# Query and output projections as three products of 16-bit halves instead of one fp32 product

## The chip, the cores and the metric

The kernel runs on one core of one Trainium2 chip. The metric is the device time of one execution in microseconds (us); lower is better. The numbers come from three timed runs of the kernel before and from one profiled execution, whose trace lists every instruction of the engines: PE (TensorE, with PEld for its weight loads), DVE (VectorE), ACT (ScalarE), POOL (GpSimd) and SP (SyncE, which here only issues DMAs).

## The reference

Two independent blocks are computed from separate inputs and joined on the last axis: block A, a state-space convolution over 2048 positions and 576 channels, and block B, attention with 32 query heads of 18 columns that share one key head and one value head. The change touches the first and the last matrix product of block B.

```python
def _B_ref(x, wq, wk, wv, wo):            # x (1, 2048, 576), wq and wo (576, 576), wk and wv (576, 18)
    ...
    q = (lambda x, *d: x.transpose(*d))((x @ wq).reshape(B, S, H, Dh), 0, 2, 1, 3)
    k = x @ wk
    v = x @ wv
    scores = jnp.einsum("bhqd,bkd->bhqk", q, k) * (Dh ** -0.5)
    p = _softmax(scores, axis=-1)
    o = jnp.einsum("bhqk,bkd->bhqd", p, v)
    return (lambda x, *d: x.transpose(*d))(o, 0, 2, 1, 3).reshape(B, S, H * Dh) @ wo
...
a = _A_ref(...)                            # kernel of 2048 taps per channel, FFT convolution, plus u * Dskip
return jnp.concatenate([a, b], axis=-1)
```

## The kernel before

**Attention.** The 2048 queries are cut into four chunks of 512 (`c`), and the 32 heads into 16 pairs (`pr`). For each chunk, two pairs form a group (`g`), and for each group the 2048 keys are walked in 16 blocks of 128 (`kb`). One step of this walk is one score tile of 128 keys by two heads of 512 queries: `scores` (L509) makes it with two 16-bit matmuls, `exponentials` (L520) turns it into `P` with one ACT instruction of 1024 elements, and `product` (L816) multiplies two such `P` tiles by the values into `ops`, in fp32. There are 1024 score tiles, and so 1024 exponentials. Score tiles have three PSUM buffers, so the scores of tile i+3 wait for the exponential of tile i. After a group, `gather` (L530) copies `ops` to SBUF and stores it to DRAM.

**Query projection.** `side` (L691) goes through 20 units (chunk c, block m of 128 query columns; the last block has 64). Unit (0, 0) is made during setup. Each other unit is `qproj` (L394): five blocks k of the 576 rows of `wq`, each for two halves of 256 queries, and for each four matmuls in fp32, one for each group of 32 output columns; the four run side by side in the array. In the trace one fp32 matmul is two passes, each with a weight load of its own (the program has 680 of these matmuls, the trace 1360). The result lies in the single PSUM bank of tag `f`, which every other piece of side work shares. DVE takes it out as `qh` and `ql`.

**Output projection.** When a chunk's eight groups are stored, `prepare` (L711) runs `normalize` (L538): denominators `dn` are loaded, inverted on DVE and stored to DRAM (`rden`), the chunk's numerators are loaded into `oT`, and for each block m of 126 rows the inverses are loaded broadcast into `db` (two buffers) and multiplied into `oT` by one DVE instruction. `outproj` (L574) then makes eight tiles (t, n) of 128 x 288, each a sum over five blocks m in fp32. The last chunk is done in parts: `outproj_part` (L600) as far as it gets beside the attention, and `finish` (L625) for what is left in `self.rest` after the last exponential.

**Convolution.** Class `Conv` makes block A in 12 chunks of 48 channels on DVE and PE: `front(k)` builds the filter (`tab`, `kg`, `ksb`), `back(k)` transforms input and filter (`hu`, `lu`, `hk`, `lk`), multiplies them (`ks`, `acc`, `pt`, `sv`, `w`) and transforms back (`iy`). Its DVE work is the larger part of what DVE does.

**What sets the order.** The order of PE, ACT and DVE is laid down while the program is built. `Clock` (L76) keeps an estimated time for each of the three engines; `Vector` (L111) and `K.pe(...)` add an estimated cost for each instruction issued. Between the scores and products of a round of three tiles, `fill` (L785) takes pieces of side work from three streams (normalization `prep`, projections `side`, convolution `conv`) as long as a credit lasts and their inputs are due. `self.due` forces a query unit in time for the heads that need it. The convolution is paced by `RATE` (1.84 us of DVE work for each step of two tiles), and what is left of it when the last exponential is issued is written out by `conv.drain()` (L894), behind everything else. Each engine then executes its list strictly in that order, whatever the real durations are.

## Time and profile before

| | us |
|---|---|
| median of three runs | 1151.15 |
| lowest and highest of the three | 1151.06, 1153.36 |
| span of the profiled execution, first to last instruction (its own time is not listed apart from the three) | 1153.0 |
| mean granted TensorE clock | 0.990 |
| first exponential starts | 26.9 |
| last exponential starts | 1127.2 |

Three things are needed to read it. The exponentials are a ruler: 1024 of them, of about 1 us each, so a stretch between two of them is a fixed part of the attention's work, and what lies behind the last one is the tail. PE's busy time counts each matmul to the end of its way through the array, so that matmuls that follow each other overlap, and busy PE is not PE at its peak. DVE executes in order, one instruction at a time, and its records overlap their neighbours by less than a tenth of a microsecond.

### The profile page before, as it was taken

To read this page: it belongs to the slowest core of one execution; us is meant where nothing else is said; L and a number is where in the kernel's file an instruction comes from. 1 tells how busy PE (TensorE), PEld (TensorE's weight loads), DVE (VectorE), ACT (ScalarE), POOL (GpSimd) and SP (SyncE) were. 2 spreads that over 40 slices of the span, in tenths; PEclk is the share of its full clock that TensorE was granted. 3 is DMA by queue.
4 is the path that set the end of the run, shared out by engine and by line. 5 is a ranking of instruction groups with operands and counts; after the bars stand their busy time and mean duration, and the time that the engine had idled before them with its cause. 6 is when DMAs were issued, how large, how long until landed. Compare 5 with 4: busy or idle time off the path is not lost.

```text
span 1153.0 us, 33012 instructions
## 1 busy us (share of the span) xinstructions
PE 1083.5 (94%) x13886; PEld 395.9 (34%) x13886; DVE 987.4 (86%) x1679; ACT 998.8 (87%) x1052; POOL 140.6 (12%) x257
## 2 busy tenths in 40 slices
PE   6999899989999999989999999999998999999998
PEld 2333233333333334323333333333332333332423
DVE  3697997998997897897799899898699799799694
ACT  2888979879989898998998899988999988899891
POOL 5232320112032000001021200001040000000000
PEclk9899999999999999999999999999999999999999
DMA  7422242114122202112222300202221301301201
GB/s 224 130 57 84 76 133 89 45 41 135 32 67 78 74 29 88 45 63 93 82 79 71 110 21 28 93 28 85 75 78 46 111 20 39 106 19 54 77 33 58
DMA packets 59279, 83.37 MB, mean 72 GB/s; under 512 B 14867, under 2 KB 35335, under 8 KB 58613
## 3 DMA queue, kind: packets, MB, share of 16 engines
q1 hardware_dynamic: 47557, 73.24, 19.4%
q0 software_dynamic: 10848, 7.37, 2.6%
q8 instruction: 111, 1.82, 0.6%
q10 hardware_dynamic: 720, 0.58, 0.2%
q14 instruction: 43, 0.35, 0.1%
HBM read 46.59 MB, written 33.85 MB: 70 GB/s over the span
## 4 chain that ended last, share of the span: by engine, by line
PE 64%; DVE 15%; ACT 14%; issue 5%; DMA 1%; SPq 0%; ACTq 0%; DVEq 0%
PE ops L823 27%; PE s L516 17%; ACT P L527 12%; PE op L193 5%; PE q L408 3%; DVE tab L119 3%; PE kg L1257 3%; PE iy L193 3%; DVE ks L119 1%; DVE acc L119 1%; DVE t L119 1%; PE hk L193 1%; PE fin L193 1%; PE lk L193 1%; DMA xr<-xT 1%
## 5 line engine op out<-in xcount | busy, mean ns | idle before, releaser
L527 ACT ACTIVATE P<-s 128x1024 f32<-128x1024 f32 x992 | 934.8, 1034 | 104.6 <-PE s L516 102.2
L823 PE MATMUL ops<-P,v_sb 128*32 128x512 f32 x4096 | 513.0, 601 | 8.5 <-DVE o L123 8.4
L516 PE MATMUL s<-aug,kaug 55*128 55x512 f16 x2048 | 309.9, 384 | 36.6 <-ACT P L527 30.7
L516 PEld LDWEIGHTS <-kaug 55*128 55x128 f16 x2048 | 92.2, 94 | 371.7 <-issue 328.5
L823 PEld LDWEIGHTS ops<-P,v_sb 128*32 128x32 f32 x4096 | 117.2, 110 | 162.6 <-issue 126.1
L458 POOL DMA_DIRECT2D qd<-qh x116 | 65.7, 573 | 323.2 <-DVE qh L127 320.6
L408 PE MATMUL q<-x,wq_sb 128*32 128x256 f32 x1360 | 84.2, 382 | 3.2 <-DVE sck L119 2.5
L193 PE MATMUL op<-wo_sb,oT 126*32 126x288 f32 (+1 forms) x1048 | 74.8, 410 | 2.6 <-DVE sck L119 1.2
L119 DVE TENSOR_TENSOR tab<-tab,tt 128x576 f32<-128x576 f32 (+1 forms) x72 | 59.1, 821 | 1.4
L123 DVE COPY ksb<-kg 128x192 f32<-128x192 f32 x48 | 17.5, 364 | 49.1 <-PE kg L1257 48.9
L119 DVE TENSOR_TENSOR tt<-fr,sum 128x576 f32<-128x576 f32 (+1 forms) x72 | 58.9, 818 | 0.0
L119 DVE TENSOR_TENSOR tab<-tab 128x576 f32<-128x576 f32 (+1 forms) x72 | 58.9, 818 | 0.0
L119 DVE TENSOR_TENSOR tab<-fr,dif 128x576 f32<-128x576 f32 (+1 forms) x72 | 58.9, 818 | 0.0
L119 DVE TENSOR_TENSOR tab<-sum,fr 128x576 f32<-128x576 f32 (+1 forms) x72 | 58.8, 816 | 0.0
L408 PEld LDWEIGHTS q<-x,wq_sb 128*32 128x32 f32 x1360 | 40.5, 110 | 43.4 <-issue 19.1
L1168 POOL MEMSET fr<- 128x192 f32 x24 | 9.8, 494 | 323.8 <-DVE tt L119 225.2
L119 DVE TENSOR_TENSOR acc<-acc,pt 128x1728 f32<-128x1728 f32 (+2 forms) x36 | 48.7, 1352 | 0.3
L119 DVE TENSOR_TENSOR pt<-us,ks 128x1728 f32<-128x1728 f32 (+2 forms) x36 | 48.2, 1351 | 0.0
L525 ACT ACTIVATE P<-s,bias 128x1024 f32<-128x1024 f32 x32 | 32.7, 1131 | 15.1 <-PE s L516 15.1
L193 PEld LDWEIGHTS op<-wo_sb,oT 126*32 126x32 f32 (+1 forms) x1048 | 29.8, 110 | 42.2 <-issue 17.4
L1257 PEld LDWEIGHTS kg<-tab 128*32 128x32 f32 x2304 | 35.5, 110 | 22.9 <-issue 7.9
L1257 PE MATMUL kg<-tab 128*32 128x64 f32 x2304 | 41.8, 221 | 1.5 <-DVE ksb L123 1.1
(160 smaller groups left out, 1018.0 us busy)
## 6 DMA issues: line engine op xcount, KB each, us to landing
od<-o SPq DMA_DIRECT2D x31, 256.0 KB
aug<-qd SPq DMA_DIRECT2D x124, 55.0 KB
u<-u SPq DMA_DIRECT2D x12, 384.0 KB
kd<-ksb SPq DMA_DIRECT2D x12, 384.0 KB
kt<-kd SPq DMA_DIRECT2D x48, 96.0 KB
outa<-u SPq DMA_DIRECT2D x12, 384.0 KB
pw<-pw SPq DMA_DIRECT2D x8, 528.0 KB
oT<-od SPq DMA_DIRECT2D x16, 252.0 KB
```

Of the source, the lines that this page charges most:

```text
L119: return self.v.tensor_tensor(out, *a, **k)
L123: return self.v.tensor_copy(out, *a, **k)
L193: nc.tensor.matmul(ps[j:e], w[:, j:e], x, start=start, stop=stop, tile_position=(0, j))
L408: nc.tensor.matmul(ps[o, 256 * f:256 * f + 256], w[:, k, i], xt[:, k, x], start=(k == 0), stop=(k == 4), tile_position=(0, 32 * j))
L458: q.dma_start(qd[h:h + n, row + d:row + d + nd, cs], src[i1:i1 + n * nd, :cs.stop - cs.start])
L516: nc.tensor.matmul(ps[:, j, :], self.kaug[r, kb * P:(kb + 1) * P], t[r, :], start=True, stop=True)
L525: nc.scalar.activation(pt, ps, AF.Exp, bias=self.bias, scale=SCALE / QQ)
L527: nc.scalar.activation(pt, ps, AF.Exp, scale=SCALE / QQ)
L823: nc.tensor.matmul(o_ps[32 * j:32 * j + 32, :], self.v[:, kb, :], pts[2 * n + j // 2][:, j % 2, :], start=(kb == 0), stop=(kb == 15), tile ...
L1168: nc.gpsimd.memset(t[:, :, 0:NF:8], one)
L1257: nc.tensor.matmul(ps[32 * g:32 * g + 32, d, :], t[:, :32], t[:, 32:], start=(j == 0), stop=(j == 1), tile_position=(0, 32 * g))
```

## The change

Both operands of the two projections are split into a 16-bit high half and a 16-bit low half (the rest after the high half is taken away), with scales `XS`, `WS` and `OS` that are taken back when the result leaves PSUM. The fp32 product becomes three 16-bit products: high x high, high x low and low x high. The halves are made on DVE by `split`, one multiplication and one subtraction for each piece; the subtraction also writes a sum, from which `guard` later decides whether the fast path is to be believed (beside the bound that was tested before).

```diff
+    def stage(self, src, name):
+        rows, n = src.shape[0], math.prod(src.shape[1:])
+        t = self.p1.tile([P, CT], F32, tag="st", name=name, bufs=2)[:rows, :n]
+        self.nc.sync.dma_start(t if len(src.shape) == 2 else t.rearrange("p (k n) -> p k n", k=src.shape[1]), src)
+        return t, self.k.t + 5.0
+
+    def split(self, src, scale, hi, lo, part=None):
+        V, n = self.V, self.summed
...
+        V.tensor_scalar(hi, src, scale, None, op0=ALU.mult)
+        V.scalar_tensor_tensor(lo, src[part], scale, hi[part], op0=ALU.mult, op1=ALU.subtract,
+                               accum_out=self.sums[part.start:part.start + src[part].shape[0], n:n + 1])
...
+    def split_x(self, c):
...
+            st = {k: self.stage(a[:, k, :], f"xs{c}_{k}") for k in range(2)}
+            for k in range(5):
+                src, ready = st[k]
+                yield "v", max(ready, self.k.t), False
+                if k < 4:
+                    self.split(src, XS, t[:, k, :], t[:, 4 + k, :])
+                else:
+                    self.split(src, XS, t[:, 8, :], t[64:, 8, :], slice(64, P))
...
     def qproj(self, c, m, xt):
-        w, nf = self.wq[m], 2 if m < 4 else 1
...
+        w, n = self.wq[m], CT if m < 4 else 256
+        terms = [x for k in range(4) for x in ((k, k), (k, 4 + k), (4 + k, k))] + [(8, 8), (9, 8)]
...
-        for f in range(nf):
-            for k in range(5):
+        for i0 in cuts:
+            part = range(i0, min(i0 + size, len(terms)))
+            for i in part:
                 for j in range(4):
...
-                    nc.tensor.matmul(ps[o, 256 * f:256 * f + 256], w[:, k, i], xt[:, k, x], start=(k == 0), stop=(k == 4), tile_position=(0, 32 * j))
-                K.pe(0.465)
...
+                    nc.tensor.matmul(ps[o, :n], w[:, terms[i][0], wc], xt[:, terms[i][1], x], start=(i == 0), stop=(i == len(terms) - 1), tile_position=(0, 32 * j))
+            K.pe(0.02 + 0.4167e-3 * n * len(part))
...
     def normalize(self, c, ms):
...
-            tiles[m] = self.p1.tile([P, CT], F32, tag="db", name=f"db{c}_{m}", bufs=2)
+            tiles[m] = self.p1.tile([P, CT], F32, tag="db", name=f"db{c}_{m}")
...
-            V.tensor_tensor(o[:mn, m, :], o[:mn, m, :], tiles[m][:mn, :], op=ALU.mult)
+            raw = raws[m][:mn, :]
+            V.scalar_tensor_tensor(raw, raw, OS, tiles[m][:mn, :], op0=ALU.mult, op1=ALU.mult)
...
+            V.tensor_scalar(o[:mn, m, :], raw, 1.0, None, op0=ALU.mult)
+            V.tensor_tensor(o[:mn, 5 + m, :], raw, o[:mn, m, :], op=ALU.subtract)
...
+    def terms(self, ps, m, t, cs, start, stop):
+        n, ts = MT[m][1], slice(t * P, (t + 1) * P)
+        for i, (a, b) in enumerate(((m, m), (5 + m, m), (m, 5 + m))):
+            matmul4(self.nc, ps, self.oT[:n, a, ts], self.wo[:n, b, cs], start=start and i == 0, stop=stop and i == 2)
...
     def outproj(self, c):
...
-                    matmul4(nc, ps, o[:mn, m, t * P:(t + 1) * P], self.wo[:mn, m, cs], start=(m == 0), stop=(m == 4))
-                    K.pe(0.485)
+                    self.terms(ps, m, t, cs, m == 0, m == 4)
+                    K.pe(0.37)
```

The last block of rows, 64 of them, holds its high and its low half in one operand of 128 rows, so a query unit has 14 products and not 15. Blocks of `x`, `wq` and `wo` no longer go straight to their place but through two staging buffers (`st`, 512 columns of fp32) that `split_x`, `weights`, `load_wo` and `normalize` use in turn (`stager_free`); `db` has one buffer. `PACE`, `RATE`, `TOTAL` and the other numbers of the planner are as they were. Over the whole program before the branch at its end, DVE has 125 more instructions; 1064 matmuls of the queries take the place of 680, and 1536 of the output (beside the attention) of 524, each new one with a weight load as an instruction of its own.

With these costs the planner puts the instructions in another order. The first place to look at is the end of DVE's list. In the kernel before, these are the rows that come last ahead of the test of the bound (`w` and `u` belong to the last convolution chunk, `part` and `oT` to the last output chunk); the chunk's `acc` and `pt` rows stand further up, between copies of `part`:

```order
L119 TENSOR_TENSOR w_14162<-sv_14161 128x2x192 x4
L119 TENSOR_TENSOR u_12568<-u_12568,dsk_12569 128x768
L119 TENSOR_TENSOR part<-part,op_1_0_1_14212 128x288
L119 TENSOR_TENSOR oT_13187<-oT_13187,db_3_14155 126x512
L119 TENSOR_TENSOR u_12568<-u_12568,iy_14232 128x384
L119 TENSOR_TENSOR u_12568<-u_12568,iy_14258 128x384
L895 TENSOR_SCALAR flag<-u_3_4_10948 1x1
```

In the changed kernel the corresponding place reads as follows, from the inversion of the last denominators on; behind these rows come two more `pt`, four more `acc`, four `sv`, four `w` and the three `u`:

```order
L129 TENSOR_SCALAR part<-op_2_1_0_15765 128x288
L129 TENSOR_SCALAR dn_21_15713<-dn_21_15713 28x128
L141 RECIPROCAL dn_21_15713<-dn_21_15713 28x128
L133 SCALAR_TENSOR_TENSOR os_3_15786<-os_3_15786,db_3_15788 126x512
L129 TENSOR_SCALAR oT_14809<-os_3_15786 126x512
L121 TENSOR_TENSOR oT_14809<-os_3_15786,oT_14809 126x512
L129 TENSOR_SCALAR part<-op_3_0_0_15793 128x288
L121 TENSOR_TENSOR ks_15571<-ks_15571 128x768
L129 TENSOR_SCALAR part<-op_3_1_0_15807 128x288
L121 TENSOR_TENSOR acc_15822<-us_15438,ks_15571 128x2304
L121 TENSOR_TENSOR pt_1_15824<-us_15438,ks_15571 128x1728
L121 TENSOR_TENSOR acc_15822<-acc_15822,pt_1_15824 128x96x18
```

The inversion of `dn`, the scaling of block 3 and the whole `acc` to `w` of the last convolution chunk now stand behind an output piece (`op_2_1_0`) that PE makes after the last scores.

The second place is PE's list from the second matmul of the last scores (`s_15_15`, made of the keys `kaug`) on. Before:

```order
L516 MATMUL s_15_15_14227<-aug_113,kaug 128x512
L193 MATMUL iy_14232<-w_14162,dft_sb 32x192 x16
L823 MATMUL ops_7_13960<-P_14_14_14203,v_sb 32x512 x2
L823 MATMUL ops_7_13960<-P_15_14_14205,v_sb 32x512 x2
L823 MATMUL ops_7_13960<-P_14_15_14207,v_sb 32x512 x2
L823 MATMUL ops_7_13960<-P_15_15_14230,v_sb 32x512 x2
L193 MATMUL iy_14258<-w_14162,dft_sb 32x192 x16
L193 MATMUL fin_14281<-wo_sb,oT_13187 32x288 x16
```

In the changed kernel, the last scores are followed by these rows:

```order
L628 MATMUL s_15_15_15756<-aug_119,kaug 128x512
L966 MATMUL ops_7_15433<-P_14_14_15725,v_sb 32x512 x2
L966 MATMUL ops_7_15433<-P_15_14_15727,v_sb 32x512 x2
L195 LDWEIGHTS oT_14809
L195 MATMUL op_2_1_0_15765<-wo_sb,oT_14809 32x288
```

Behind them stand eleven more pairs for `op_2_1_0`, the last four products, 24 pairs for `op_3_0_0` and `op_3_1_0`, then both `iy`, then `fin`: the inverse transform, which stood ahead of the last four products, now stands behind all the work that is left beside the attention, and the 21 block products left for `fin` became 24.

227 lines of the change are left out of this document (163 added, 64 removed).

## The prediction

> **What bounds the kernel now.** I read the page first (engine lines, then the chain), then the busy time of each stretch of 64 exponentials, then the rows of the operations that change.
>
> ```profile
> PE 1083.5 (94%) x13886; PEld 395.9 (34%) x13886; DVE 987.4 (86%) x1679; ACT 998.8 (87%) x1052; POOL 140.6 (12%) x257
> PE 64%; DVE 15%; ACT 14%; issue 5%; DMA 1%; SPq 0%; ACTq 0%; DVEq 0%
> L527 ACT ACTIVATE P<-s 128x1024 f32<-128x1024 f32 x992 | 934.8, 1034 | 104.6 <-PE s L516 102.2
> ```
>
> PE carries most of the chain, and the exponentials wait 102.2 us for scores: PE is what is late most often. But three engines stand at 86% or more, and an average hides where each is the limit. The stretches show it (start:end, length, then busy us of PE, PEld, DVE, ACT, POOL).
>
> ```profile
> core 0: us, PE busy (x) PEld busy (x) DVE busy (x) ACT busy (x) POOL busy (x), PEclk, DMA share, GB/s
> 0.00:100.10 100.10, 87.28 (x1054) 31.58 (x1054) 63.58 (x139) 68.93 (x73) 36.46 (x71) 0.95 0.45 134
> 100.10:177.30 77.20, 68.84 (x782) 24.00 (x783) 74.79 (x125) 68.33 (x70) 19.56 (x32) 0.96 0.31 100
> ...
> 383.70:450.70 67.00, 65.08 (x822) 23.77 (x818) 65.28 (x102) 60.38 (x65) 0.59 (x1) 1.00 0.12 39
> ...
> 656.60:722.80 66.20, 65.48 (x832) 24.08 (x828) 64.20 (x101) 60.40 (x65) 0.61 (x1) 1.00 0.11 33
> ...
> 863.20:925.80 62.60, 57.22 (x692) 18.86 (x689) 55.48 (x94) 59.91 (x66) 0.83 (x2) 1.00 0.23 76
> 925.80:997.10 71.30, 69.67 (x954) 26.21 (x954) 63.85 (x97) 60.55 (x64) 0.83 (x2) 1.00 0.14 47
> 997.10:1061.10 64.00, 61.36 (x712) 20.50 (x701) 61.11 (x101) 59.97 (x66) 0.00 (x0) 1.00 0.16 52
> ...
> 1127.20:1153.00 25.80, 20.19 (x316) 10.58 (x312) 9.22 (x17) 1.79 (x3) 0.00 (x0) 0.95 0.18 65
> ```
>
> In four of the 15 stretches between the first and the tail (100, 384, 657 and 997 us) DVE is busy for 95 to 97%: there DVE sets the pace. In the others it has room, and the length follows PE: from the stretch at 863 to the one at 926, PE's busy time rises by 12.45 us and the length by 8.7, so 0.70 us for each us of PE. The tail from the last exponential on is 24.8 us long (it starts at 1127.2 and runs 1.0), and DVE has only 9.2 us to do in it.
>
> **The change on PE.** Rows of the chain, as pieces in order of time (start, length), give the pace of the array without the pipeline's ends.
>
> ```profile
> 53.29 1.00 PE q L408 x16
> ...
> 63.02 1.43 PE q L408 x24
> ```
>
> ```profile
> 1081.00 0.75 PE s L516 x6
> ...
> 1119.41 0.49 PE op L193 x8
> ...
> 1126.82 0.32 PE s L516 x2
> ```
>
> Eight more q passes cost 0.43 us; four run side by side, so a group of 256 fp32 columns takes 0.215 us for each pass. Four more 16-bit score matmuls, side by side in twos, also cost 0.43: 512 columns in 0.215 us, twice the fp32 pace. A group of 288 fp32 columns takes 0.49 / 2 = 0.245 us, and in 16 bits, by the pace of the scores, 288/512 of 0.215 = 0.121.
> A query unit had 20 groups (5 blocks, 2 halves, 2 passes), 4.30 us; it gets 14 of 512 columns, 3.01. That is 1.29 less for 15 units and half of it for the four narrow ones: 22.0 us. A block of an output tile goes from 0.49 to 0.363. Beside the attention 131 of them become 128: 64.2 to 46.5, 17.7 us less. In the tail 21 become 24: 10.3 to 8.7. So PE gives up **39.7 us** ahead of the last exponential and 1.6 behind it.
>
> No row shows 16-bit matmuls in groups of four. What is nearest:
>
> ```profile
> L1257 PE MATMUL kg<-tab 128*32 128x64 f32 x2304 | 41.8, 221 | 1.5 <-DVE ksb L123 1.1
> ```
>
> That is 576 groups of four short passes, each pass with a load of its own, in 41.8 us: 73 ns a group. Groups of 121 and 215 ns therefore have time for their loads. The bound on the other side is that a pass gains nothing from 16 bits; I take the score row, which is of that type.
> [...]
>
> **The change on DVE.** Groups by line, with shapes kept apart:
>
> ```profile
> L131 DVE SCALAR_TENSOR_TENSOR ql<-q,qh 128x512 f16<-128x512 f32 x15 | 10.4, 692 | 0.5
> L127 DVE TENSOR_SCALAR qh<-q 128x512 f16<-128x512 f32 x15 | 10.3, 686 | 11.3 <-PE q L408 11.3
> L135 DVE TENSOR_REDUCE ab<-qh 128x1 f32<-128x512 f16 x15 | 10.1, 676 | 0.0
> L119 DVE TENSOR_TENSOR oT<-oT,db 126x512 f32<-126x512 f32 x16 | 10.9, 682 | 0.0
> L127 DVE TENSOR_SCALAR stage<-stage 128x2112 f32<-128x2112 f32 x2 | 2.5, 1250 | 0.0
> ```
>
> A subtraction of 512 columns costs 0.69 us. The multiplication that rounds to 16 bits reads SBUF and has no row: between 0.36 (1250 ns for 2112, plus a start) and the 0.69 of qh, which reads PSUM. I take 0.36, since the stage row reads SBUF too. Then `x` costs 16 pairs at 1.05 and one of four slabs at 3.4: 20.2. `wq` costs 6.7 (five blocks of 512 + 128 columns, the last half as wide), `wo` 6.7 (512 + 64), five reductions of 0.68 and nine small operations 4.8, and the scaling 19 times two more (0.69 + 0.36): 20.0. Three additions into `part` go, 1.3. The sum is 57.1; neighbours overlap by 0.08 (the part row below starts 0.37 ahead of the next and lasts 0.45), 125 times, so **+48 us**, and +63 if the multiplications take 0.69. Of that, the order puts behind the last exponential what was ahead of it before: about 19.5 us. So DVE has 29 us more to do while the attention runs, and some 19 more behind it.
> [...]
>
> **While the attention runs.** In the 11 stretches that PE sets, its cut brings 39.7 x 11/15 x 0.70 = 20.4 us. In the four that DVE sets it brings nothing, and DVE's addition costs 29 x 4/15 / 0.97 = 8.0. So the last exponential ends 12.4 us earlier, at 1128.2 - 12.4 = 1115.8. The ends: 39.7 earlier if PE sets all, 8 later if the cut brings nothing.
> The loads of `x`, `wq` and `wo` now pass SP's queue in 32 pieces, each of which waits there until DVE has split the piece two ahead of it, and with it what stands behind, such as the loads of `aug` for the next heads. I price this at nothing: the stretches above use 0.31 of the DMA engines or less, and convolution work stands between a load and its split. Where that cover is missing, DVE waits for a landing (2.9 us for 126 KB, below).
>
> **The tail.** DVE's and PE's timeline of before (start, length):
>
> ```profile
> 1104.90 0.45 DVE L123 COPY part<-op 128x288 f32<-128x288 f32 x1
> 1105.27 0.95 DVE L119 TENSOR_TENSOR ks<-ks 128x768 f32<-128x768 f32 x1
> 1106.26 2.56 DVE L119 TENSOR_TENSOR acc<-us,ks 128x2304 f32<-128x2304 f32 x1
> ...
> 1113.20 0.21 DVE L127 TENSOR_SCALAR dn<-dn 28x128 f32<-28x128 f32 x1
> 1113.44 0.94 DVE L139 RECIPROCAL dn<-dn 28x128 f32<-28x128 f32 x1
> ...
> 1123.31 1.96 DVE L119 TENSOR_TENSOR w<-sv 128x384 f32<-128x384 f32 x4
> ```
>
> ```profile
> 1127.08 1.51 PE L193 MATMUL iy<-w,dft_sb 128*32 128x192 f32 x32
> 1128.40 1.90 PE L823 MATMUL ops<-P,v_sb 128*32 128x512 f32 x16
> 1130.12 1.48 PE L193 MATMUL iy<-w,dft_sb 128*32 128x192 f32 x32
> 1131.41 3.10 PE L193 MATMUL fin<-wo_sb,oT 126*32 126x288 f32 x48
> ```
>
> From acc's start to w's end DVE needed 19.0 us; without the six part operations between (0.37 each) and the inversion (1.1), 15.7. All of it now stands behind `op_2_1_0`, which stands behind a product (two tiles) that needs the last exponential but one. Counted from the end of the last exponential: that product starts some 1.0 earlier, takes 0.9 (half of the ops row above) and op_2_1_0 0.36 more, so it is done at +0.3; its copy (0.45) and the inversion (0.21 + 0.94) end at +1.9. The next DVE instruction needs the inverses back from DRAM, and everything is queued behind it. The trace has that trip:
>
> ```profile
> L553 SPq DMA_DIRECT2D rden<-dn x7: 328/334/348, 331.9 to 1114.4; - x7
> ```
>
> ```profile
> L563 SPq DMA_DIRECT2D db<-rden x19: 640/758/785, 333.5 to 1115.8; - x19
> ```
>
> ```profile
> qd<-qh POOLq DMA_DIRECT2D x6, 126.0 KB, 2.9
> ```
>
> 1.4 us lie between the two issues, and a DMA of half its size lands 2.9 after issue on POOL's queue: about 4.6, so +6.5. Then the scaling's three operations (1.7), copies and ks (1.7), and acc to w (15.7): +25.6. Both `iy` with one evacuation between take 3.4 (1.5 + 0.6 + 1.3): +29.0. From fin's start to the span's end were 1153.0 - 1131.4 = 21.6, now 1.6 less: **+49.0 us** in place of 24.8. Before, all this ran under the last 20 exponentials; that cover is gone.
>
> **The sum.** 1115.8 + 49.0 = 1164.8 against the span of 1153.0. The span is 1.85 above the median of 1151.15, so 1163.0.
>
> **Rivals.** (1) PE sets every stretch: of DVE's 987.4 us, 914.6 lie between the first stretch (63.6) and the tail (9.2); with 29 more they fit, at 97%, into 973 of the 1027 that it had. Then the attention ends 39.7 earlier and the result is 1163.0 - 27.3 = 1135.7, **faster**. It decides from the point where PE's cut is worth over 24.2 us ahead of the last exponential, the tail's price. For it speaks the 102.2 us that ACT waits for PE; against it that four stretches have DVE full already, and all 29 us come on top. (2) DVE sets the whole second half: the cut brings nothing and DVE costs 8 us, 1183; at the upper price of the multiplications 15 more, and with ten of the staged loads late by 1 us, ten more. (3) The 16-bit groups are held up by issue or loads and run like fp32 passes: a query unit 6.0 us in place of 4.3, an output block 0.73 in place of 0.49, 29 us more for 17 units and 37 for 152 blocks. 60 of them ahead of the last exponential, at 0.70, make 42 us in place of the 12.4 gained, and fin some 7: about 1225. The kg row speaks against it.
>
> **How the numbers follow.** Forecast, 1154 to 1176: 0.62. Rival 2 and beyond, to 1195: 0.13. Rival 3: 0.02. Rival 1 or most of it, below 1148.8: 0.16. Between, 1148.8 to 1153.5 (0.2% either way, about what a measurement can tell from no change): 0.07. That is faster 0.16, same 0.07, slower 0.77. The range, 1143 to 1184, takes in rival 2 and three quarters of the way to rival 1; some 0.15 is left out.
>
> **What would show it.** Right: the last exponential starts near 1115; behind it a DVE row `acc` of 2.56 us and a wait of some 5 us before `os`; `iy` starts 25 us after the last exponential. q's chain pieces of 8 matmuls at 0.43 (two groups of 512). Stretches at 97% DVE more often than four. Wrong: a last exponential ahead of 1104, DVE with room everywhere; or q groups well over 0.215 us.

## The result, and the profile after

| | before | after |
|---|---|---|
| median of four runs each, us | 1151.11 (1151.0 to 1153.36) | 1198.86 (1198.24 to 1199.09) |
| span of the profiled execution | 1153.0 | 1196.5 |
| mean granted clock | 0.990 | 0.971 |
| first to last exponential ("main part" below) | 1100.3 | 1115.2 |
| from the start of the last exponential to the end ("tail") | 25.8 | 54.8 |

The ratio is 1.0405, 95% interval 1.0389 to 1.0421: 47.7 us slower, where 12 had been forecast. The sign was right, the size was not, and the range (to 1184) does not hold the time.

From the page of the changed kernel: the engines, the chain, and the groups of the exponentials, the value products and the scores (busy us, mean ns | idle time before, and what ended it).

```profile
PE 1063.1 (89%) x14198; PEld 391.0 (33%) x14198; DVE 1045.3 (87%) x1841; ACT 996.8 (83%) x1052; POOL 139.4 (12%) x257
PE 46%; DVE 29%; ACT 13%; issue 8%; DMA 3%; SPq 0%; DVEq 0%; ACTq 0%
L639 ACT ACTIVATE P<-s 128x1024 f32<-128x1024 f32 x992 | 932.9, 1036 | 122.9 <-PE s L628 121.2
L966 PE MATMUL ops<-P,v_sb 128*32 128x512 f32 x4096 | 518.5, 606 | 16.1 <-DVE o L125 16.1
L628 PE MATMUL s<-aug,kaug 55*128 55x512 f16 x2048 | 317.1, 386 | 52.4 <-ACT P L639 46.5
```

PE gave up work, and the exponentials wait for scores longer, not shorter: 121.2 us, where it was 102.2. PE itself waits twice as long for DVE to copy `o` out of the bank of the value products (8.4 before). DVE's share of the chain has gone from 15% to 29%.

The stretch from the first exponential to the last, and the tail, of the kernel before and then of the changed one (length, then busy us of PE, PEld, DVE, ACT, POOL; granted clock):

```profile
26.90:1127.20 1100.30, 1046.11 (x13418) 380.19 (x13418) 969.43 (x1641) 990.36 (x1041) 126.87 (x229) 0.99 0.22 68
1127.20:1153.00 25.80, 20.19 (x316) 10.58 (x312) 9.22 (x17) 1.79 (x3) 0.00 (x0) 0.95 0.18 65
```

```profile
26.50:1141.70 1115.20, 1022.58 (x13574) 371.72 (x13574) 1002.94 (x1771) 988.45 (x1041) 127.69 (x233) 0.98 0.23 68
1141.70:1196.50 54.80, 22.32 (x472) 13.79 (x464) 33.72 (x48) 1.79 (x3) 0.00 (x0) 0.73 0.10 36
```

DVE has 33.5 us more to do in the main part and 24.5 more in the tail. The main part became 14.9 us longer, where I had made it 12.4 shorter.

The pieces of the changed kernel that the sums on PE and DVE rested on, first from the chain (start, length), then from the groups by shape:

```profile
436.49 1.95 PE op L195 x60
605.67 3.13 PE q L519 x56
```

```profile
L129 DVE TENSOR_SCALAR xh<-xs 128x512 f16<-128x512 f32 x16 | 6.7, 421 | 0.9 <-DMA xs<-xT 0.8
L133 DVE SCALAR_TENSOR_TENSOR xh<-xs,xh 128x512 f16<-128x512 f32 x12 | 8.3, 692 | 0.4
L133 DVE DVE_READ_ACCUMULATOR xh<-xs,xh 128x1 f32 x12 | 1.0, 82 | 0.0
```

A query unit (14 groups) takes 3.13 us with its start, an output tile (15 groups) 1.95: 0.22 and 0.13 a group, close to the 0.215 and 0.121 of the forecast. The rounding multiplication takes 0.42, where I had taken 0.36, and each sum that the subtraction writes is a row of its own, of 0.08. So the pieces are about those of the forecast. The rows of the two projections give up 42.4 us of PE's busy time (q 84.2 to 59.3, op 77.6 to 60.1). In the main part PE's busy time fell by only 23.5, though: matmuls that the change does not touch were busy longer (scores 309.9 to 317.1, value products 513.0 to 518.5). The half clock told of at the end may be part of that; it was not followed up.

Waits of this length for a copy of `o` are new in the changed kernel (the longest was 2.3 us before). From its timeline (start, length, what the engine waited for):

```profile
799.60 1.95 DVE L121 TENSOR_TENSOR acc<-acc,pt 128x1728 f32<-128x1728 f32 x1
800.33 1.03 PE L966 MATMUL ops<-P,v_sb 128*32 128x512 f32 x8
801.46 0.95 DVE L121 TENSOR_TENSOR tab<-tab,tt 128x768 f32<-128x768 f32 x1
802.33 0.68 DVE L129 TENSOR_SCALAR qh<-q 128x512 f16<-128x512 f32 x1
...
804.57 0.68 DVE L125 COPY o<-ops 128x512 f32<-128x512 f32 x1
...
805.31 1.08 PE L966 MATMUL ops<-P,v_sb 128*32 128x512 f32 x4 [3.94 <-DVE o L125]
```

A group's last product is done at 801.4. Its copy stands on DVE behind two convolution pieces and the evacuation of a query unit (`qh` and the three small rows behind it), and starts 3.2 us later; the next product needs that one bank, and the next scores stand behind it in PE's list. Counted over the whole main part, PE stands still for 1.2 us or more 6 times before (9.6 us in all) and 14 times after (29.1 us).

The loss is not spread evenly. Of the 14.9 us, 13.5 lie in one stretch of 64 exponentials, which took 62.6 us before (863 to 926 us, quoted in the prediction); the others, some longer and some shorter, add up to the rest.

```profile
866.40:942.50 76.10, 62.36 (x592) 17.67 (x584) 63.34 (x112) 65.55 (x70) 8.34 (x15) 0.91 0.22 70
```

Neither PE (82%) nor DVE (83%) is full in it. PE stands still four times for 1.8 to 2.6 us, and behind each of these waits the granted clock is at 0.5 for 3.4 us. In the 15 stretches, DVE is busy for 95% or more in two, where it had been four before: the forecast's sign of a DVE that is full more often did not come.

### The profile page after: what moved, and what is told of

Read it like the earlier page. It is cut to its first block, busy times and chain, and to the rows that moved or that the text cites. A ratio compares the mean times of both kernels' runs of the same rounds, so it can differ in the third digit from the quotient of the medians.

```text
span 1196.5 us, 33819 instructions
## 1 busy us (share of the span) xinstructions
PE 1063.1 (89%) x14198; PEld 391.0 (33%) x14198; DVE 1045.3 (87%) x1841; ACT 996.8 (83%) x1052; POOL 139.4 (12%) x257
## 4 chain that ended last, share of the span: by engine, by line
PE 46%; DVE 29%; ACT 13%; issue 8%; DMA 3%; SPq 0%; DVEq 0%; ACTq 0%
PE ops L966 19%; PE s L628 12%; ACT P L639 12%; DVE tab L121 6%; DVE ks L121 3%; DVE acc L121 3%; PE kg L1396 2%; PE q L519 2%; PE iy L195 2%; DVE pt L121 2%; PE op L195 2%; DVE t L121 2%; DVE tt L121 1%; DVE fr L121 1%; PE hu L195 1%
## 5 line engine op out<-in xcount | busy, mean ns | idle before, releaser
L639 ACT ACTIVATE P<-s 128x1024 f32<-128x1024 f32 x992 | 932.9, 1036 | 122.9 <-PE s L628 121.2
L966 PE MATMUL ops<-P,v_sb 128*32 128x512 f32 x4096 | 518.5, 606 | 16.1 <-DVE o L125 16.1
L628 PE MATMUL s<-aug,kaug 55*128 55x512 f16 x2048 | 317.1, 386 | 52.4 <-ACT P L639 46.5
L966 PEld LDWEIGHTS ops<-P,v_sb 128*32 128x32 f32 x4096 | 111.2, 110 | 177.2 <-issue 145.6
L195 PE MATMUL op<-wo_sb,oT 126*32 126x288 f16 (+1 forms) x1536 | 55.9, 293 | 13.6 <-DVE part L129 9.6
L519 PE MATMUL q<-xh,wq_sb 128*32 128x512 f16 (+1 forms) x1064 | 59.3, 363 | 4.3 <-DVE wq_sb L129 2.3
L195 PEld LDWEIGHTS <-oT 126*32 126x32 f16 (+1 forms) x1824 | 48.2, 98 | 36.2 <-issue 26.3
L195 PE MATMUL iy<-w,dft_sb 128*32 128x192 f32 x768 | 40.0, 344 | 18.4 <-DVE w L121 17.7
L125 DVE COPY ksb<-kg 128x192 f32<-128x192 f32 x48 | 17.4, 362 | 42.0 <-PE kg L1396 42.0
```

The lines of the kernel that those rows point to most:

```text
L125: return self.v.tensor_copy(out, *a, **k)
L195: nc.tensor.matmul(ps[j:e], w[:, j:e], x, start=start, stop=stop, tile_position=(0, j))
L519: nc.tensor.matmul(ps[o, :n], w[:, terms[i][0], wc], xt[:, terms[i][1], x], start=(i == 0), stop=(i == len(terms) - 1), tile_position=(0, ...
L628: nc.tensor.matmul(ps[:, j, :], self.kaug[r, kb * P:(kb + 1) * P], t[r, :], start=True, stop=True)
L639: nc.scalar.activation(pt, ps, AF.Exp, scale=SCALE / QQ)
L966: nc.tensor.matmul(o_ps[32 * j:32 * j + 32, :], self.v[:, kb, :], pts[2 * n + j // 2][:, j % 2, :], start=(kb == 0), stop=(kb == 15), tile ...
```

## The experiments

All sixteen runs, in the order in which they ran (four, four, four, two, two). "First" is the start of the first exponential; main part and tail as above, from the profiled execution. Ratios are to the kernel before on the same chip.

| run | time, us | ratio, 95% | first | main | tail |
|---|---|---|---|---|---|
| e1 no split work, new order | 1203.15 | 1.0405 to 1.0472 | 34.4 | 1115.4 | 51.3 |
| e2 four products, new order | 1222.89 | 1.0558 to 1.0639 | 26.4 | 1136.1 | 57.4 |
| e3 one product, new order | 1189.81 | 1.0281 to 1.0346 | 26.0 | 1109.6 | 52.2 |
| e4 halves for nothing | 1182.59 | 1.0216 to 1.0285 | 34.1 | 1126.9 | 19.2 |
| e5 PE's cut, old order | 1150.26 | 0.9978 to 1.0002 | 27.1 | 1095.7 | 24.1 |
| e6 before, DVE far ahead | 1179.33 | 1.0225 to 1.0270 | 26.4 | 1132.6 | 17.9 |
| e7 after, DVE near | 1207.96 | 1.0463 to 1.0517 | 27.1 | 1095.6 | 82.9 |
| e8 after, tail interleaved | 1193.46 | 1.0341 to 1.0393 | 26.7 | 1114.7 | 50.0 |
| e9 DVE's part alone | 1196.14 | 1.0354 to 1.0390 | 27.3 | 1124.2 | 40.8 |
| e10 DVE work, old order | 1180.44 | 1.0216 to 1.0259 | 26.0 | 1126.0 | 26.1 |
| e11 all but DVE's work | 1173.79 | 1.0152 to 1.0199 | 27.9 | 1123.9 | 19.2 |
| e12 before, DVE near | 1159.13 | 1.0033 to 1.0069 | 25.7 | 1110.6 | 21.1 |
| e13 DVE's part and PE's cut | 1185.38 | 1.0277 to 1.0351 | 26.6 | 1116.0 | 38.4 |
| e14 warm tail, 55 rows | 1201.95 | 1.0406 to 1.0460 | 26.3 | 1114.0 | 60.3 |
| e15 warm tail, fp32 | 1199.19 | 1.0388 to 1.0446 | 25.5 | 1115.0 | 57.3 |
| e16 warm tail, 126 rows | 1194.75 | 1.0349 to 1.0406 | 25.0 | 1114.5 | 54.0 |

### One engine's work changed, the new order kept (e1, e2, e3)

The first question was which engine's work the main part follows. The planner's costs stay as in the changed kernel, so every engine's list keeps its order, and only the work of one engine changes.

```diff
 e1, in split (and likewise in normalize and for the reductions)
-        V.tensor_scalar(hi, src, scale, None, op0=ALU.mult)
-        V.scalar_tensor_tensor(lo, src[part], scale, hi[part], ...)
+        self.k.dve(hi, 0.58e-3, src)
+        self.k.dve(lo, 1.04e-3, src[part], hi[part])
 e2, in terms (and likewise in qproj)
-        for i, (a, b) in enumerate(((m, m), (5 + m, m), (m, 5 + m))):
+        for i, (a, b) in enumerate(((m, m), (5 + m, m), (m, 5 + m), (5 + m, 5 + m))):
 e3, in terms (and likewise in qproj)
+        for i, (a, b) in enumerate(((m, m),)):
```

> The changed kernel with every engine's order kept to the instruction, but the splits' instructions on DVE left out (halves of x and of both weights, the two extra operations of each scaling, three reductions): 57.5 us of DVE by the durations of the changed kernel's rows, nearly all ahead of the last exponential. The products read constants in place of the halves, so the output is not the reference's. THEORY (DVE, which executes in order, sets the pace almost everywhere, and PE's cut was turned into waits): the last exponential starts 25 to 50 us earlier than in the changed kernel (1092 to 1117 in place of 1141.7), total 1150 to 1175. RIVAL 1 (PE still sets most stretches, as I forecast; its cut was merely outweighed): at most 10 us earlier, total above 1188. RIVAL 2 (the new order itself costs the time, whatever the instructions in it last): within 5 us, above 1193.

> The changed kernel, order and DVE work kept, with PE's cut given back: the fourth product (low by low) is made too, and the query units get two groups with zero weights beside it, so that a query unit has 20 groups and an output block four. By 0.215 and 0.121 us a group that is 37.4 us more PE work ahead of the last exponential and 2.9 behind it. THEORY (DVE sets the pace): the added work falls into PE's waits; last exponential at most 10 us later, total 1200 to 1212. RIVAL 1 (PE sets, 0.70 us for each us of PE work): 26 us later and 3 in the tail, about 1228. RIVAL 2 (order): within 5 us and the tail's 3, 1199 to 1207.

> The changed kernel, order and DVE work kept, with one product (high by high) in place of three, so that the low halves are not used in the output: 63.9 us less PE work ahead of the last exponential, 5.8 behind it. THEORY (DVE sets the pace): last exponential at most 15 us earlier, total 1180 to 1199. RIVAL 1 (PE sets, 0.70): 45 us earlier and 6 in the tail, about 1148. RIVAL 2 (order): within 5 us, 1190 to 1199.

```profile
34.40:1149.80 1115.40, 1022.75 (x13574) 372.47 (x13574) 950.03 (x1623) 988.13 (x1041) 124.83 (x227) 0.98 0.22 67
```

This row of e1 (the main part) stands beside the changed kernel's: DVE has 52.9 us less to do, PE and ACT the same, and the main part is 0.2 us longer. My theory fell with it; what came is rival 2, the order. Even the long stretch stays (73.2 us in place of 76.1). (The first exponential starts 7.9 us late, which is a blemish of the run and is told at the end.) In e3, 63.9 us less on PE by the pieces' pace (52.2 of busy time) took 5.6 us off the main part, all of it in the first stretch. But in e2, 37.4 us more on PE (29.8 of busy time) added 20.9, nearer to rival 1 than to the theory's 10 at most. So in this order taking work away, from either engine, brings 0 to 0.1 us for each us; adding it to PE costs 0.56 (0.70 for each us of busy time). That doesn't look like the limit of one engine. My reading, which no run shows by itself: with one list each for DVE and PE, tied together by single PSUM banks, the other engine is late as soon as one gets faster.

### Each half of the change in the old order (e5, e10)

The same question put to the kernel before, whose order is kept: e5 makes only PE's products cheaper, e10 only adds DVE work.

```diff
 e5, in qproj: 14 groups spread over the ten pieces of a unit, K.pe(0.465) kept
-  nc.tensor.matmul(ps[o, 256 * f:256 * f + 256], w[:, k, i], xt[:, k, x], ...)
+  for i in range(14 * u // (5 * nf), 14 * (u + 1) // (5 * nf)):
+      nc.tensor.matmul(ps[32 * j:32 * j + 32, :n], self.cst[:, 32 * j:32 * j + 32], self.cst[:, :n], ...)
 e10, in Clock.filled, called behind each evacuation
+        if self.calls > 40 and self.calls % 4 == 0 and self.left:
+            self.left -= 1
+            self.extra()
```

> The kernel before, every engine's order kept to the instruction and no work added on DVE, but the products of both projections in 16 bits: 14 groups in place of 20 for a query unit, three in place of two fp32 passes for an output block; the weights and x are a constant in their place, so the output is not the reference's. PE has about 40 us less to do ahead of the last exponential, at no price. The first four runs left one theory, the ORDER: in the changed kernel it is not the amount of work on DVE or PE that sets the main part, but an order in which evacuations of PSUM stand behind convolution pieces on DVE, so that PE waits, and after such waits gets the half clock. By it PE's cut is worth something in the old order: last exponential 10 to 25 us earlier than before (1102 to 1117), total 1125 to 1140. RIVAL (PE's cut is worth nothing in any order, since ACT and DVE are late at the same places anyway): last exponential at most 5 us earlier, total 1144 to 1151.

> The kernel before, every engine's order kept to the instruction, with 50 pairs of a rounding multiplication and a subtraction of 512 columns added on DVE, each behind an evacuation of PSUM, one for each fourth of them, uncounted by the planner and read by nothing: 55 us by the changed kernel's rows (0.42 and 0.69). If DVE's AMOUNT of work costs by itself: 25 to 55 us, total 1176 to 1207. If only the ORDER costs, as the run without split work seemed to say: within 8 us, 1144 to 1160.

e5, from its page: engines, chain, and the same groups as above.

```profile
PE 1049.6 (92%) x14198; PEld 388.2 (34%) x14198; DVE 986.3 (86%) x1679; ACT 997.1 (87%) x1052; POOL 141.5 (12%) x258
PE 44%; DVE 36%; ACT 9%; issue 6%; DMA 3%; SPq 1%; POOL 0%; DVEq 0%; ACTq 0%
L527 ACT ACTIVATE P<-s 128x1024 f32<-128x1024 f32 x992 | 933.2, 1034 | 104.6 <-PE s L516 101.0
L829 PE MATMUL ops<-P,v_sb 128*32 128x512 f32 x4096 | 511.2, 599 | 15.2 <-DVE o L123 15.1
L516 PE MATMUL s<-aug,kaug 55*128 55x512 f16 x2048 | 314.8, 383 | 52.5 <-ACT P L527 40.0
```

At no price on DVE the whole cut is worth 4.7 us of the main part, and the total can't be told from no change: it lies where the rival had it, and 10 us above the range of my theory. (The first stretch of 64 exponentials got 3.6 us longer, 103.7 in place of 100.1, because loads of `x` that no longer wait for PE stand ahead of the `aug` loads of the next heads, for which PE waits 5.8 us; behind that stretch the cut is worth 8.1.) PE's busy time fell by 34 us, and the exponentials wait for scores as before, 101.0 us. So PE's amount of work alone does not make the scores late. They stand in its list behind products that wait for DVE, longer now than before (15.1 us and 8.4); that is a part of it, and the rest of the 101 us was not taken apart. DVE's share of the chain goes from 15% to 36% without one instruction more.

e10 is the mirror. Its main part grew by 25.7 us for some 48 us more of busy DVE (1017.2 in place of 969.4), so 0.54 for each us, and the chain reads:

```profile
DVE 43%; PE 43%; ACT 7%; issue 5%; DMA 1%; POOL 0%; DVEq 0%; ACTq 0%; SPq 0%
```

So DVE's amount of work does cost by itself. e1 does not contradict that: there the order had been laid down for more work, and taking the work out did not close the gaps.

The added pairs start at 253.7 us, so what lies ahead of them is a control. The second and the third stretch take 77.1 and 65.7 us, as before (77.2 and 65.7). The first, with the same instructions, does not:

```profile
0.00:95.90 95.90, 83.86 (x1054) 30.53 (x1054) 63.57 (x139) 68.81 (x72) 36.45 (x71) 1.00 0.47 139
```

It ends 4.2 us earlier than before (quoted in the prediction: 100.1 us, clock 0.95), 0.9 of it because the first exponential starts earlier. The kernel before spent 10.2 us of that stretch at the half clock, e10 nothing. So two executions can differ by some 3 us in the first stretch alone. Behind it, e10 grew by 29.0 us for 48.1 us more of DVE, 0.60 for each us.

### How far DVE may run ahead (e6, e7, e12)

The planner lets convolution pieces stand on DVE ahead of PE by an allowance that grows with the convolution's lag behind its pace. I suspected that the lag, which the splits cause, costs by way of this allowance.

```diff
 e6, before: ahead = AHEAD + 1.0     e7, after: ahead = AHEAD     e12, before: ahead = AHEAD
-        ahead = AHEAD + min(max(lag, 0.0) / 20.0, 1.0)
```

> The kernel before, complete and with fp32 products, but with the planner's allowance for DVE (by how much its queue may run ahead of PE) set to 1.7 us throughout, the value that it reaches by itself in the changed kernel, where the convolution lags 30 to 47 us behind its pace by the planner's own count (2 to 9 in the kernel before, allowance 0.8 to 1.2). THEORY (ORDER, by this allowance): the last exponential starts 15 us or more later than 1127, long PE waits appear, and PE's clock is at half in more places; total above 1165. RIVAL (the allowance is harmless; the order suffers from something else): total within 6 us of before, 1146 to 1158.

> The changed kernel, complete, with that allowance held at 0.7 us, however far the convolution lags. THEORY (ORDER, by this allowance): the waits of PE for copies of o and for evacuations shrink and the last exponential starts 15 to 30 us earlier (1112 to 1127 in place of 1141.7); more of the convolution is left for the tail, which grows by 20 to 28 us; total 1185 to 1207. RIVAL: last exponential no earlier than 1137, total above 1215.

> The kernel before, complete, with the allowance by which DVE may run ahead of PE held at 0.7 us in place of 0.8 to 1.2. In the changed kernel that made the main part 19.5 us shorter and the tail 28 longer. If DVE has room enough here, the main part gets 2 to 10 us shorter and nothing is left for the tail: 1142 to 1150. RIVAL (DVE needs its pieces early, so that what is gained in PE's waits is lost in waiting for convolution pieces): 1151 to 1165.

The allowance matters as much as the theory said: 1.7 us throughout makes the kernel before 32 us longer in the main part, and 0.7 makes the changed one 19.6 shorter there. But e7 pays it back in the tail, which grows by 28.1 us, since DVE does 985 us of work in the main part in place of 1003 and the rest behind it. e12 is slower than before, as its rival had it. So in the changed kernel the allowance decides where DVE's added work is paid: the one other setting that was tried does not give the time back. And e6 shows that an order alone can cost 27 us in total, with no work added on any engine.

### DVE's part alone, and PE's cut on top (e9, e13); all but DVE's part (e4, e11)

e9 adds the splitting instructions, counted by the planner, to the kernel before; e13 keeps e9's order and makes the products 16-bit. e4 and e11 are the changed kernel planned without the splits; e11 repeats e4 without a blemish in its setup.

```diff
 e9, in side and in normalize (and a like stream for wo)
+                for k in range(5):
+                    self.split(xts[c][:, k, :])
+                    yield "v", 0.0, False
...
             V.tensor_tensor(o[:mn, m, :], o[:mn, m, :], tiles[m][:mn, :], op=ALU.mult)
+            V.tensor_scalar(self.hi[:mn, :], o[:mn, m, :], 1.0, None, op0=ALU.mult)
+            V.tensor_tensor(self.lo[:mn, :], o[:mn, m, :], self.hi[:mn, :], op=ALU.subtract)
 e13: e9 with the matmuls of e5
 e4, e11, in split
-        V.tensor_scalar(hi, src, scale, None, op0=ALU.mult)
-        V.scalar_tensor_tensor(lo, src[part], scale, hi[part], ...)
```

> DVE's part of the change alone: the kernel before with its fp32 products, its loads and its buffers, to which the splitting instructions are added (20 pairs for x, ten each for the two weights, two operations behind each scaling, three reductions: 58 us), written to a scratch tile that nothing reads, and counted by the planner, which lays the order down with them. THEORY (the price of the change is DVE's work with the order that it brings, and PE's cut is worth 2 to 5 us): total 1187 to 1207, in the main part or behind it. RIVAL (staged loads, the single buffer for the inverses and the smaller pieces of PE work cost most of it): at most 1175.

> DVE's part alone (1196.1 us) once more, its order kept to the instruction on every engine, but the products of both projections in 16 bits with a constant in place of the weights and of x (the output is not the reference's), so that PE has some 40 us less to do. Loads and buffers are those of the kernel before, and x is still read by DVE, so its loads wait as before; in the first trial of PE's cut they did not, which put the first stretch 3.6 us off. If the change is DVE's part plus a PE cut that becomes waits: 1188 to 1195. RIVAL (in an order that is short of DVE, the cut is worth nothing at all): 1195 to 1198. RIVAL (the cut pays once DVE's pieces are planned for): below 1185. What the changed kernel (1198.9) takes above this run is then the price of its staged loads, its single buffer for the inverses and its larger remainder of convolution.

> PE's part of the change alone: as the first of these runs, the splits' work on DVE left out (constants in place of the halves, so the output is not the reference's), but now the planner doesn't count it either and lays the order down anew; it then has no convolution work left for the time behind the last exponential. THEORY (DVE sets the pace; PE's cut is worth little by itself): last exponential 1105 to 1125, tail 24 to 32 us, total 1130 to 1155, so at most 20 us better than the kernel before although PE has 41 us less to do. RIVAL 1 (PE sets 11 of 15 stretches): 20 us or more from the main part and the tail's 1.6: 1129 or less. RIVAL 2 (order): here, too, the main part is no shorter than before, 1150 or more.

> The run on halves for nothing once more, without its blemish (large tiles of constants written by GpSimd during setup put the first exponential 7.5 us off and held up the first query stores): the changed kernel with staged loads, single buffer, 16-bit products and an order laid down without the splits, one small tile of constants in place of the operands (the output is not the reference's). THEORY (DVE's work is the price): first exponential near 27, total 1140 to 1158. RIVAL (staged loads, buffers and smaller PE pieces cost by themselves): 1165 or more, with long PE waits early on, behind loads.

Main part and tail of e9, and of e13:

```profile
27.30:1151.50 1124.20, 1048.20 (x13402) 379.77 (x13405) 1014.58 (x1783) 990.22 (x1042) 128.57 (x230) 0.99 0.21 67
1151.50:1192.30 40.80, 24.09 (x332) 11.91 (x324) 23.23 (x35) 1.75 (x3) 0.00 (x0) 0.84 0.11 41
```

```profile
26.60:1142.60 1116.00, 1014.42 (x13622) 372.33 (x13625) 1014.01 (x1782) 988.33 (x1042) 128.69 (x231) 0.99 0.21 67
1142.60:1181.00 38.40, 20.39 (x424) 12.60 (x416) 23.57 (x35) 1.75 (x3) 0.00 (x0) 0.84 0.12 44
```

DVE's part alone, with the order laid down for it, costs 43.3 us (1196.14 against 1152.86), nearly the whole of the change; between the profiled executions it is 23.9 in the main part and 15.0 in the tail. PE's cut on top gives 8.2 back in the main part (5.6 of it behind the first stretch) and 2.4 in the tail, so that e13 comes out between its theory and the rival by which the cut pays. The sums fit the changed kernel, the places do not: e9 and e13 take 62 us in the stretch in which the changed kernel takes 76.1, and lose their time elsewhere. So they show what DVE's work with an order of its own costs, and not that the changed kernel pays it at the same places. What the changed kernel takes above e13 lies in the tail (54.8 against 38.4): it left 10 us more of DVE's work for it (33.72 against 23.57), and the last scaling's trip through DRAM.

e4 and e11 went against the theory: without any split work, but with staged loads and a new order, the kernel still takes 21 us more than before. e11's lengths show where: its first five stretches of 64 exponentials take 401.6 us, before 383.7, and the chain in the first of them reads

```profile
55.49 3.77 DMA wos<-wo
...
59.28 3.02 DMA wos<-wo
...
62.32 2.60 DMA wos<-wo
...
65.84 2.67 DMA aug<-qd
...
68.55 1.44 PE s L626 x5
```

Staged loads of `wo` that wait for each other in SP's queue stand ahead of the `aug` loads of the next heads, and PE waits 5.1 us for those. In the changed kernel this place shows no such wait, and its first five stretches take 378.6. So the price of the staged loads is shown for e11, not for the change. Most of what e11 loses besides lies in its third stretch, 80.6 us in place of 65.7. There PE waits 10.1 us for copies of `o`, once for 7.0 us, until DVE is through a run of convolution pieces; from the chain:

```profile
190.75 0.61 DVE o L125
191.41 3.64 PE ops L962 x16
```

So such waits can cost this much without any split work on DVE: that is the order again.

### The tail (e8, e14, e15, e16)

```diff
 e8, in main, behind each step of the last normalization
                 prep.advance()
+                conv.drain(6)
 e14, in back, ahead of the last iy (e15: 20 groups of dft_sb, fp32, 128 rows; e16: 34 groups of oT, 126 rows)
+                warm = self.at.ps_s.tile([P, 2, CT], F32, tag="s", name="warm")
+                for i in range(50):
+                    matmul4(nc, warm[:, i % 2, :], self.at.kaug[0:55, 0:P], self.at.kaug[0:55, 0:CT])
```

> The changed kernel, complete, with one thing moved behind the last exponential: the rest of the convolution (acc, pt, sv) stands on DVE ahead of the last scaling, whose inverses are on their way through DRAM meanwhile, in place of behind it. Main part unchanged. If the trip through DRAM and what waits behind it is a term of the tail of its own, as I forecast: 5 to 9 us less, total 1190 to 1194. RIVAL (the tail is DVE's amount of work and PE's half clock): within 2 us, 1197 to 1201.

> The changed kernel, complete, with 50 groups of four 16-bit matmuls of 512 columns added in PE's list ahead of the first iy of the tail, into a free score bank that nothing reads: 10.75 us at the full clock, within the 15.4 us that PE waits there for w. If the half clock behind long waits is a term of its own: the granted clock is 1.0 when iy starts, iy's first 32 matmuls go from 2.8 to 1.5 us, total 1195.5 to 1198. RIVAL (the clock falls for another reason, or costs nothing here): iy as before, 1198 to 1200.

> The changed kernel, complete, with 20 groups of four fp32 matmuls of 512 columns and 128 rows in the place where the run before had 50 groups of 16-bit matmuls on 55 rows, which kept PE busy for 21.5 us and left the granted clock at 0.5. If the clock follows how much of the array works (rows, or passes), it rises within some 4 us: the stream takes 10 to 11 us, ends inside the 15.4 us wait, and iy's first 32 matmuls take 1.5 us in place of 2.8; total 1196 to 1198.5. If the clock follows nothing of the kind in this place: 17 us, total 1200 to 1203.

> The same place, 34 groups of four 16-bit matmuls of 512 columns on 126 rows, so that only the rows differ from the 55-row stream that left the clock at half. If rows decide: the clock rises within some 4 us, the stream takes 9 to 10 us, iy 1.5 us, total 1196 to 1198.5. If it is the type, and 16-bit work alone does not raise the clock: 14.6 us at half clock (0.43 a group), iy 2.8 us as in the changed kernel, total 1198 to 1200.

The tail of the changed kernel, from its timeline (the last exponential ends at 1142.7):

```profile
1144.96 0.94 DVE L141 RECIPROCAL dn<-dn 28x128 f32<-28x128 f32 x1
...
1151.44 0.69 DVE L133 SCALAR_TENSOR_TENSOR os<-os,db 126x512 f32<-126x512 f32 x1 [5.54 <-DMA db<-rden]
...
1155.08 2.55 DVE L121 TENSOR_TENSOR acc<-us,ks 128x2304 f32<-128x2304 f32 x1
...
1169.39 1.96 DVE L121 TENSOR_TENSOR w<-sv 128x384 f32<-128x384 f32 x4
1170.09 2.79 PE L195 MATMUL iy<-w,dft_sb 128*32 128x192 f32 x32 [15.43 <-DVE w L121]
...
1173.54 1.65 PE L195 MATMUL iy<-w,dft_sb 128*32 128x192 f32 x32 [0.67 <-DVE u L121]
1175.02 2.38 PE L195 MATMUL fin<-wo_sb,oT 126*32 126x288 f16 x72
```

Every step of the forecast's walk is there, in its order. In e8 DVE works while the inverses travel, and the tail is 4.8 us shorter, as the 5.5 us wait let expect. The first `iy` takes 2.79 us, the second 1.65, since PE comes out of its long wait with the granted clock at 0.5. e14's stream, at half the clock throughout, took 21.5 us in place of 10.75 and ended 4.8 us behind `w`; `iy` still took 2.79, and the tail grew by 5.5 us. e15 kept PE busy up to `iy`, whose first half then took 1.48; but its groups took twice what I had reckoned (0.86 us at the full clock, since an fp32 group of 512 columns is two passes: the trace has 160 rows for the 80 matmuls, and four side by side every 0.43 us), so its stream ended late and the total gained nothing. e16's stream ended 5.6 us ahead of `iy`, and the clock had fallen again (0.62 from 1168 to 1172; `iy` took 2.79). So this clock is worth 1.3 us here, and no run turned it into time. e16's total lies 4 us below the changed kernel's, but its tail only 0.8; I read nothing into it.

## Why the prediction was wrong, step by step

**PE's and DVE's new work: right in the pieces, DVE's 10 us short.** The 16-bit groups run at their columns' pace (0.22 us for 512 columns and 0.13 for 288, by the chain rows above; at the pace of fp32 passes it would be 0.43 and 0.245), so rival 3 is out. DVE's added work came out at 57.9 us of busy time, where the forecast had 48 after overlap. Before overlap it is 62.5 (the durations of all DVE rows added up) in place of 57.1, since the multiplication takes 0.42 and each written sum 0.08; and overlap takes 4.6 off, not 9. PE's pieces were right, while its busy time in the main part fell by 23.5 in place of 39.7, as told above.

**"In the 11 stretches that PE sets, its cut brings 39.7 x 11/15 x 0.70 = 20.4 us": this step failed.** The cut is worth 4.7 us of the main part in the old order (e5; 8.1 behind the first stretch) and 8.2 in an order with DVE's work in it (e13). The 0.70 came from two stretches, at 863 and at 926 us, in which PE's busy time differs by 12.45 us and the length by 8.7. In the same two rows, quoted in the prediction, DVE's busy time goes from 55.48 to 63.85: by 8.4. They allow the other reading just as well. Nor do the rows divide the stretches between two engines: in those at 384 and 657 us, which I gave to DVE, PE is busy for 97 and 99%. And a stretch in which DVE isn't full isn't one that PE sets: in e5, PE gave up 34 us of busy time, and the exponentials waited for scores as long as before.

**"DVE's addition costs 29 x 4/15 / 0.97 = 8.0": failed as well, by the same thought.** DVE got 33.5 us more in the main part, near the 29 of the forecast, but it is not only in four stretches of 15 that this costs time. DVE's part alone made the main part 23.9 us longer (e9), and spread over the old order 25.7 (e10), half a us or more for each us. In e10 the eleven stretches that I took to be PE's grew by 23.2 us for 39.3 more of DVE, and the four that I took to be DVE's by 5.8 for 8.8. Together: -8.2 + 23.9 = +15.7, measured +14.9, forecast -12.4; that the sum fits so well is in part luck, since the places differ. These two terms are 27.3 of the 32 us by which the span missed the forecast. How much of DVE's price is its work and how much the order that comes with it stays open: work without a new order cost 27.6 us (e10), an order without work 27.2 (e6), and the new order kept its price when the work was taken out (e1).

**The tail: right in its mechanism, 4.8 us short (53.8 from the end of the last exponential, forecast 49.0).** The inversion ends at +3.2 in place of +1.9, behind three `ks` pieces; the trip through DRAM takes 5.5 in place of 4.6; acc to w 16.3 in place of 15.7; with smaller ones, w is done 3.0 us late. The two `iy` add 0.3, with the first at half the clock, and what runs from `fin`'s start on 1.5. e8 shows that the trip is a term of its own. (The rest of the miss, 4.2 us, lies between spans and medians: the span was 1.9 above the median before, 2.4 below it after. In every other run the span is 1.7 to 2.2 us shorter than the time of its own execution, so by estimate the profiled execution of the kernel before took some 1154.8, 3.6 above the median.)

**The rivals.** Rival 1 is out: even free of charge, the cut is worth about a third of the 24.2 us from which it would have decided. Rival 2 had the direction (the cut brings little), but priced DVE at 8 as the forecast did. The range ended where it did because DVE's price in the main part had no upper end of its own; with the cut worth nothing and all of the 29 us on the path, it is 1163 + 20.4 + 21 = 1204.

## What to carry to other kernels

Where three engines stand at 86% or more and hand work on through single buffers, a cut on the busiest can be worth little (here 0.1 to 0.2 us per us), while work added to PE or DVE cost half of its length or more (nothing was added to ACT): price what is added first, and bound it from above by its whole length. A slope read from two stretches is one only if the other engines' rows stay the same between them. Before moving work from one engine to another, take the price apart: products made cheaper without their preparation, in the old order (e5), and the preparation without its use (e10 in the old order, e9 with an order planned for it), gave these prices in one run each. Then compare stretch by stretch: a sum that fits can hide that the time is lost in different places.

## What the runs showed of the hardware

**The granted clock of PE follows more than being busy.** In 4 us windows of e14, the stream of 16-bit matmuls on 55 rows, which began at 1153.2; and of e16, on 126 rows, begun at 1152.3 (length, PE, PEld, DVE, ACT, POOL, clock, DMA share, GB/s):

```profile
1160.00:1164.00 4.00, 4.00 (x44) 1.52 (x40) 3.93 (x5) 0.00 (x0) 0.00 (x0) 0.50 0.02 4
...
1172.00:1176.00 4.00, 4.00 (x48) 1.58 (x44) 0.00 (x0) 0.00 (x0) 0.00 (x0) 0.50 0.01 4
```

```profile
1152.00:1156.00 4.00, 4.00 (x48) 1.79 (x40) 3.86 (x4) 0.00 (x0) 0.00 (x0) 0.50 0.00 0
1156.00:1160.00 4.00, 4.00 (x68) 1.93 (x64) 3.93 (x3) 0.00 (x0) 0.00 (x0) 0.83 0.02 4
1160.00:1164.00 4.00, 2.31 (x44) 1.00 (x36) 3.93 (x5) 0.00 (x0) 0.00 (x0) 1.00 0.00 0
```

21.5 us without a pause on 55 rows left the clock at half; the same type and size on 126 rows had it at full after some 5 us, and so had fp32 on 128 rows (e15: its stream began at 1153.1, and the clock was 0.50 from 1152 to 1156, 0.73 in the next 4 us and 1.00 from 1160 on). The operands' values differ between e14 and e16 as well, so that rows decide is likely, and not shown by itself. In the main part the changed kernel spent some 41 us at the half clock and the kernel before some 20 (twice the length times one minus the granted clock, in windows of 2 us). In the trace of the changed kernel, of its 14 waits of 1.2 us or more, the seven of 1.8 to 3.9 us were followed by half clock, and the seven of 1.2 to 1.75 us were not; but one of 1.15 us, ended at 507.9, was (clock at 0.5 for 3.4 us from 508.3 on), so the length of the wait alone does not decide. What it costs there can be read from one place only: the first stretch took 3.3 us less in e10, without the 10.2 us at half clock of the kernel before.

**One instruction on DVE took 11.4 us beside writes of GpSimd.** In e1, beside the tiles of constants that GpSimd wrote from 3.6 to 17.3 us:

```profile
5.99 11.39 DVE L129 TENSOR_SCALAR ab<-ab 128x48 f32<-128x48 f32 x1
```

The same instruction took 0.19 us in the kernel before and in the changed one. The `tensor_tensor` just ahead of it in e1 took 0.26 us beside the same writes, as before, so not every instruction is held. This is the blemish of e1 and e4, whose first exponentials start 8 us late (34.4 and 34.1); in e11, with one small tile of constants in their place, the first starts at 27.9. The row ends at 17.4 us, as the other's burst does (17.3); that the writes held it is my reading of these times, and by what means is not shown.
